# Attention then an MLP-mixer block on one core: when the second batch element's x is turned, where attention lies beside its token mixing, and two small reorderings

## The chip, the core and the metric

The kernel runs on one core of a Trainium2 chip. The core has TensorE (PE, with the weight load PEld beside it), VectorE (DVE), ScalarE (ACT), GpSimd (POOL) and SyncE (SP), whose queue issues nearly all DMAs. Each engine works through its own instructions in the order of the program, and waits by semaphores for the others. The metric is the device time in microseconds; a run's time is told beside the span of its profile.

## The reference

All in float32. First attention with normalized queries and keys, for 8 batch elements, 12 heads, 448 positions and 64 channels per head; then a mixer block on the result, which has 768 channels.

```python
q_n, k_n = (rmsnorm(q, g_q), rmsnorm(k, g_k))
scores = scale * np.matmul(q_n, k_n.transpose(0, 1, 3, 2))
attn = np.exp(scores - max); attn = attn / (sum(attn) + 1e-09)
out = np.matmul(attn, v)                      # (8, 12, 448, 64)

x = out.transpose(0, 2, 1, 3).reshape(8, 448, 768)
xt = x.transpose(0, 2, 1)
h = np.maximum(xt @ w_tok1, 0.0) @ w_tok2     # token mixing: 448 -> 256 -> 448
u = x + h.transpose(0, 2, 1)
h2 = np.maximum(u @ w_ch1, 0.0) @ w_ch2       # channel mixing: 768 -> 1536 -> 768
out = u + h2
```

## The kernel before

**Elements and pairs.** The work goes by batch element b = 0..7. Two heads make a pair, p = 0..47, six to an element; two pairs make a step group t = p // 2. While the mixer of element b runs, attention of element b + 1 runs beside it (`AHEAD = 1`). All instructions of PE, DVE, ACT and POOL stand in an order that the program itself writes out; only SP's queue is ordered by the framework. Work is kept in lists of items, each with a cost in us and a function that issues its instructions. `merge` (L27) weaves several lists into one in proportion to their costs; `run` issues them. `later(us, fn)` puts a function off until items of that cost have been run; the DMAs of x are issued so.

**Attention.** `att_step(g)` (L585) lists the items of step g; g = 4t + s, four steps s = 0..3 to a group of two pairs. The function `tiled` holds PE's part: `score` (L387, with the exponential of L391 on ACT), `values` (L460). After it stand, on DVE, `denominators` (at s = 0, L489 to L506, which write the attention result into `uT`), `group_sums` (L428: partial sums of the exponentials, 128x896), loads, then `behind` (reductions and roots for later pairs) and `turns`. `turns` are `turn_qk` (L361 to L369): queries and keys of the next pairs are transposed, on PE for pairs below 12 (`pre.plain`), on DVE above (L364), and the queries are multiplied by g on ACT (L367). At s = 2 pair n = 2t + 2 is turned, at s = 3 pair n + 1. Scores of step 4(t + 1) need both. From group `BIG` = 9 on attention is laid in larger blocks, `big_step`.

**Normalization.** `Start.square` (L1262 for pairs below 12, L1265 above) squares a pair's queries and keys on ACT into a buffer `sq`; `Start.reduce` (L1279) sums them on DVE. There are three such buffers: `sq_1` for pairs 1 and 3, `sq_2` (the front of the large tile `hb`) for 5 and 7, and `sq` for all others. `hb` holds queries and keys of the first pairs, and later the hidden layer of the channel mixing. `roots` makes inverse square roots by Newton steps, for pairs 2 to 11 on POOL (L1309 to L1312). `scale` (L349, DVE) applies them.

**x.** Token mixing needs x with positions on the partitions. For b > 0 `trans_x` (L744) transposes each of six blocks of `uT` in squares of 32 on DVE, three to a half; `send_x` (L712) writes a half with four DMAs into a DRAM buffer `xs`, 2 to 8 us later by the items' clock, and `load_x` (L719) reads it back 12 us later. `x_items(b, h)` lists half h. The buffer `xt` holds both halves and shares its memory with the sums `tu` of the channel mixing.

**Mixer.** `tok1` (L758) is the first product of the token mixing, four times four matmuls of 128x384, evicted by ACT (L761) into h1; `tok2` (L766) the second, six times two of 128x448, added into `uT` by DVE (L771). Both take turns in two PSUM banks, `m_ps`. The first halves of h1 come from x's half 0, the second from half 1. `moving_sums` make T1, T2 on DVE (L787, L788) and T3, T4 on POOL (L789, L790). Channel mixing of elements 1 to 7 uses seven products of quarter matrices in place of eight (`ch1` L882, 21 items; `ch2` L939, 21 items). Its weights come in units from DRAM (`load_units`, L813), some of which are sums of weight quarters.

**Element 0 prepares the weights.** In element 0 each of 36 weight stages is loaded (`raw`), converted on DVE and ACT (L263 to L308, five to six instructions, the last being L308), stored (L192) and used at once by `first_stage` (L854, four matmuls of 128x448); every sixth stage of the second layer is evicted by ACT and added to `uT` by POOL (L864). The sums of weights are made on POOL (L204 to L207): `some` for the first eight stages, `direct` for the last six from their stage tiles, and `sums`, 25 items that load, sum and send the other stages in turn. POOL's order behind the last stage is: six `direct` sums, two `sums`, the two L864 of the last stage, further `sums`, T3 and T4.

**Order around the change.** In element 0, attention steps 13 to 24 are merged with element 0's mixer; x's half 0 of element 1 is turned between steps 22 and 23. Then `last` is run: x's half 1, the last six stages, `direct`, `sums[:5]` and two output transposes (`turns`, L975, sent by L702). In element 1 `tok1` of half 0 is run with two more output transposes; then `tok1` of half 1, `tok2` and `ch1`, merged with `sums[5:20]`, are all woven into attention steps 25 to 36. From element 2 on attention blocks begin only with the first `ch1`.

The lines that decide this order:

```python
begin, early = merge(tok1_items(b, 1) + early[:3 * KC], left[2:]), early[3 * KC:]
if b == 1:
    early, double = merge(begin + early, sums[5:20]), merge(double, sums[20:])
    begin = []
early = begin + early + double
...
att = att_items(lo, lo + 10) + x_items(b + AHEAD, 0) + att_items(lo + 10, lo + per - (b == 1 and not shifted))
...
last = x_items(1, 1) + merge(last, direct + sums[:5], turns(b, y_order(b)[2:4]))
...
run(merge(att, early) + last)
```

`shifted` is a second form of the program, for large gains g, which does not run with these inputs.

Of the kernel before, what the change touches and what calls it, by code (L numbers as in the profile page):

```python
# [44 lines left out]
def whole(ctx, tc, shifted, pre, q, k, v, g_q, g_k, moe_w_tok1, moe_w_tok2, moe_w_ch1, moe_w_ch2, out):  # L45
# [386 lines left out]
    def on_pe(p):  # L432

        return shifted or p < NPAIR
# [150 lines left out]
    def att_step(g):  # L585


        t, s = divmod(g, 4)
        p = 2 * t
        pair = (p, p + 1)  # L590
        live = g < NG
        items = []

        def finish():
            if s == 0 and t:
                last = (p - 2, p - 1)
                for k in (NK - 2, NK - 1):
                    values(last, k)
            if live:
                for k in ((0,), (1, 2), (3, 4), (5, 6))[s]:  # L600
                    score(t, k)
            if s == 0 and t:
                if not on_pe(p - 1):
                    row_sums(t - 1)
                for i in last:
                    st.pop(("v", i))

        def tiled():
            if shifted:
                if live:  # L610
                    both_shifted()
            else:
                finish()
            if live and s == 3:
                for i in pair:
                    st.pop(("qkT", i))
            if inside:
                for fn in turns:
                    fn()
            if live and s and not shifted:  # L620
                for k in ((), (0,), (1, 2), (3, 4))[s]:
                    values(pair, k)

        def both_shifted():
            i = p + s // 2
            if s % 2 == 0:
                score_shifted(i)
                return
            for k in range(NK):
                values((i,), k)  # L630
            for k in range((NK + 1) // 2):
                st.pop(("e1", i, k))
            st.pop(("v", i))
            for part in denominators((i,)):
                part()

        n = p + 2
        ahead, behind, turns = [], [], []  # L640
        f = lambda fn, *pairs: [lambda i=i: fn(i, st) for i in pairs]
        scales = lambda n: [lambda i=i: scale(i) for i in (n, n + 1)]
        if g in (1, 5):
            ahead, behind = f(pre.square, g // 4 * 2 + 4), f(pre.reduce, g // 4 * 2 + 4)
        elif g in (2, 6):
            ahead, behind = f(pre.square, g // 4 * 2 + 5), f(pre.reduce, g // 4 * 2 + 5)
        elif g in (3, 7):
            behind = pre.roots(g // 4 * 2 + 4, st)
        elif g in (4, 8):
            behind = scales(g // 4 * 2 + 2)  # L650
        if live and n < NP:
            late = n < 2 * NPAIR + 2
            if t >= NPAIR // 2 and late:
                if s == 1:
                    ahead, behind = f(pre.square, n), f(pre.reduce, n) + f(pre.square, n + 1)
                elif s == 2:
                    behind = f(pre.reduce, n + 1) + pre.roots(n, st) + scales(n)
            elif t >= NPAIR // 2:
                a, b = f(pre.square, n) + f(pre.reduce, n), f(pre.square, n + 1) + f(pre.reduce, n + 1)
                behind = (a, b + pre.roots(n, st), scales(n), [])[s]  # L660
            now = {2: [] if pre.plain(n) else [n], 3: [n, n + 1] if pre.plain(n) else [n + 1]}.get(s, [])
            turns = [lambda q=q, i=i: turn_qk(q, i) for q in now for i in (1, 0)]

        inside = g < 2 * NPAIR
        items += [(0.3, fn) for fn in ahead]
        items.append((2.4 if s == 1 else 3.2, tiled))
        part = lambda fns, c=0.4: [(c, fn) for fn in fns]
        if s == 0 and t and not shifted:
            items += part(denominators((p - 2, p - 1)))
        if live and not on_pe(p):  # L670
            items += [(0.5, lambda k=k: group_sums(t, k)) for k in ((), (1, 2), (3, 4), (5, 6))[s]]

        if s == 0 and 5 < p + 1 < NP:
            items.append((0.0, lambda: load_v(p + 1)))
        if live and s == 1 and 5 < p + 2 < NP:
            items.append((0.0, lambda: load_v(p + 2)))
        js = []
        if live and s == 0:
            js = [n, n + 1] if pre.plain(p) else [n + 1]
        elif live and s == 3 and not pre.plain(n):  # L680
            js = [n + 2]
        items += [it for j in js if pre.first_slot + 2 <= j < NP
                  for it in part(pre.loads(j, st, nc.sync, nc.sync), 0.2 if pre.plain(j) else 0.6)]
        if g == 3:
            items += [it for j in (6, 7) for it in part(pre.loads(j, st, nc.sync, nc.sync), 0.2)]
        items += part(behind)
        if not inside:
            items += part(turns)
        if g == 4 * BIG - 1 and not shifted:
            items += part(pre.loads(n + 3, st, nc.sync, nc.sync), 0.3)  # L690
        return items
# [285 lines left out]
    def turns(b, cs, send=True):  # L977

        def one(cc):
            trans_y(b, cc)  # L980
            if send:
                later(2.0, lambda: send_y(b, cc, st.pop(("y", cc))))
        return [(0.3, lambda cc=cc: one(cc)) for cc in cs]

    def y_order(b):

        return [o * KC + m for m in ((0, 1, 2) if b else (2, 0, 1)) for o in range(2)]
# [6 lines left out]
    def x_items(b, h):  # L994
        return [(0.1, lambda j=j: trans_x(b, j)) for j in range(h * NC // 2, (h + 1) * NC // 2)]
# [108 lines left out]
    for b in range(B):  # L1104
        early, double = middle_items(b)
        if b == 0:
            early, last = first_items(
                tok1_items(0, 0) + x_items(0, 1) + tok1_items(0, 1) + early, double, some)
        else:
            if b > 1 and in_next(b - 1):  # L1110

                y, z = sends(b - 1, y_order(b - 1)[:4]), left
                left = [y[0], y[1], z[0], y[2], z[1], y[3]]
            run(merge(tok1_items(b, 0), left[:2]))
            begin, early = merge(tok1_items(b, 1) + early[:3 * KC], left[2:]), early[3 * KC:]
            if b == 1:
                early, double = merge(begin + early, sums[5:20]), merge(double, sums[20:])
                begin = []
            early = begin + early + double
            early, last = early[:-4], early[-4:]  # L1120
        lo = (b + AHEAD) * per + 1
        att = []
        if b + AHEAD < B and (shifted or b < 2):
            att = att_items(lo, lo + 10) + x_items(b + AHEAD, 0) + att_items(lo + 10, lo + per - (b == 1 and not shifted))
            if b and not shifted:
                ahead, block, beside, between = big_step(BIG, False)
                att += ahead + [block] + beside + between
        elif b + AHEAD < B:
            t = (b + AHEAD) * NPAIR // 2
            blocks = [big_step(t + i // 2, i % 2) for i in range(1, NPAIR + 1)]  # L1130
            blocks[4][3].extend(x_items(b + 1, 0))
            early = place(early, blocks, [near(early, at) for at in BLOCKS])
        if b == 0:
            last = x_items(1, 1) + merge(last, direct + sums[:5], turns(b, y_order(b)[2:4]))
        else:
            if b + 1 < B:
                last = merge(last, x_items(b + 1, 1))
            last += last_items(b)
        run(merge(att, early) + last)
        if b == 0:  # L1140
            load_units(0)
        left = turns(b, y_order(b)[4:])
# [5 lines left out]
class Start:  # L1148
# [105 lines left out]
    def square(self, p, st):  # L1254
        x, d = self.by_rows(p, st["qk", p])
        rows, n = x.shape[0], x.shape[1]
        if self.plain(p):

            parts = ((0, n),) if p else ((0, n // 2), (n // 2, n))
            sq = (self.sq_1 if p in (1, 3) else self.sq_2 if p in (5, 7) else self.sq)[0:rows]  # L1260
            for lo, hi in parts:
                self.nc.scalar.activation(out=sq[:, lo:hi, 0:d], in_=x[:, lo:hi], func=AF.Square)  # L1262
        else:
            sq = self.sq[:].rearrange("p r d -> p (r d)")[:, 0:n * d].rearrange("p (r d) -> p r d", d=d)
            self.nc.scalar.activation(out=sq, in_=x, func=AF.Square)  # L1265
        st["sq", p] = sq
# [130 lines left out]
```

## Time and profile before

| what | us |
|---|---|
| median of three runs | 1317.32 (1316.29 to 1317.63) |
| the profiled execution | 1318.47 |
| its span | 1316.7 |
| PE busy | 1269.7 |
| PE, channel mixing L882 and L939 | 201.8 + 150.7 and 339.6 |
| PE, scores L387 and values L460 | 145.4 and 132.7 |
| PE, token mixing L758 and L766 | 86.4 and 75.5 |
| DVE, partial sums L428: 90 of 1.219 | 109.7 |

The page gives one profiled execution. Lines are those of the kernel before; a group is named by line, engine, operation, and output and input tiles. "xN" counts instructions; a float32 matmul shows as two. A busy PE is not PE at its peak: its records stretch where the granted clock is lower. The chain that ended last is 75% PE and 2% DMA. In slices of a fortieth of the span PE is at 9 tenths or more but for the first, third, eighth, ninth and last:

```
PE   5989999889999999999999999999999999999997
DVE  6887688927774366644666267644666356433212
```

Element 0's mixer runs from about 85 to 271 us, element 1's from 271 to 440, and each of the next takes some 150 us.

### The profile page before, as it was taken

How to read it: one execution, taken by the hardware profiler on the slowest of the kernel's cores; microseconds unless marked ns; L12 is line 12 of the kernel's file. 1: busy time of each engine (PE TensorE's matmuls, PEld its weight loads, DVE VectorE, ACT ScalarE, POOL GpSimd, SP SyncE). 2: the span in 40 equal slices, each digit the busy share in tenths (PEclk: the TensorE clock that was granted, in tenths of full speed). 3: DMA queues.
4: the chain of work that ended last, by engine and by line, in shares of the span. 5: the costliest groups of instructions: out<-in, count | busy, mean ns of one | idle time of the engine just before them, and what ended most of it. 6: DMA issues, size and time to landing. Idle time of an engine off the chain costs nothing.

```text
span 1316.7 us, 20214 instructions
## 1 busy us (share of the span) xinstructions
PE 1269.7 (96%) x7408; PEld 933.5 (71%) x7408; DVE 763.8 (58%) x1205; ACT 372.6 (28%) x740; POOL 355.0 (27%) x575
## 2 busy tenths in 40 slices
PE   5989999889999999999999999999999999999997
PEld 3444444436788677796778767886787868797997
DVE  6887688927774366644666267644666356433212
ACT  5553333212332044302432033312333033200100
POOL 1203230355563122321232123321232123111220
PEclk9998999999999999999999999999999999999999
DMA  9664577889889767695648767585766964386554
GB/s 210 167 182 117 147 191 188 211 207 243 247 217 212 194 159 172 153 239 103 164 136 207 168 139 181 138 230 112 180 161 152 223 137 131 118 219 134 179 169 93
DMA packets 502449, 228.06 MB, mean 173 GB/s; under 512 B 374532, under 2 KB 464004, under 8 KB 502340
## 3 DMA queue, kind: packets, MB, share of 16 engines
q1 hardware_dynamic: 489218, 224.83, 68.6%
q10 hardware_dynamic: 12994, 1.84, 0.8%
q8 instruction: 61, 1.00, 0.3%
q14 instruction: 48, 0.39, 0.1%
q0 software_dynamic: 128, 0.00, 0.0%
HBM read 187.07 MB, written 39.52 MB: 172 GB/s over the span
## 4 chain that ended last, share of the span: by engine, by line
PE 75%; DMA 2%; DVE 1%; SPq 1%; POOL 0%; issue 0%; ACT 0%; DVEq 0%; POOLq 0%; ACTq 0%
PE m_ps L882 25%; PE m_ps L939 25%; PE s_ps L387 7%; PE o_ps L460 7%; PE m_ps L758 5%; PE m_ps L766 5%; PE d_ps L440 1%; DMA unit<-ws 1%; DMA x<-xs 0%; DMA qk_t<-in_k_dram 0%; DMA ws<-raw 0%; SPq L702 0%; DVE es L428 0%; DVE ms L1279 0%; DVE nt L1321 0%
## 5 line engine op out<-in xcount | busy, mean ns | idle before, releaser
L939 PE MATMUL m_ps<-hb,unit 128*128 128x224 f32 x1764 | 339.6, 353 | 2.2 <-DMA unit<-ws 1.5
L939 PEld LDWEIGHTS m_ps<-hb,unit 128*128 128x128 f32 x1764 | 332.2, 190 | 13.3 <-issue 10.9
L882 PE MATMUL m_ps<-tu,unit 128*128 128x224 f32 x1008 | 201.8, 355 | 0.3 <-DVE hb L887 0.3
L882 PEld LDWEIGHTS m_ps<-tu,unit 128*128 128x128 f32 x1008 | 189.0, 190 | 14.8 <-issue 8.5
L391 ACT ACTIVATE e<-s_ps 128x448 f32<-128x448 f32 x294 | 138.4, 549 | 188.2 <-PE s_ps L387 179.4
L387 PE MATMUL s_ps<-qkT 64*64 64x448 f32 x1260 | 145.4, 549 | 7.0 <-ACT qkT L367 4.2
L882 PE MATMUL m_ps<-uT,unit 128*128 128x224 f32 x756 | 150.7, 353 | 0.0
L882 PEld LDWEIGHTS m_ps<-uT,unit 128*128 128x128 f32 x756 | 142.5, 190 | 5.0 <-issue 4.1
L460 PE MATMUL o_ps<-e,v 64*64 64x448 f32 x1148 | 132.7, 547 | 0.1
L428 DVE TENSOR_TENSOR es<-es,e 128x896 f32<-128x896 f32 x90 | 109.7, 1219 | 19.6 <-ACT e L391 14.7
L948 POOL TENSOR_TENSOR uT<-uT,r 128x448 f32<-128x448 f32 (+1 forms) x56 | 57.8, 1041 | 231.4 <-DVE r L948 143.6
L887 DVE TENSOR_TENSOR r<-m_ps,r 128x448 f32<-128x448 f32 x63 | 39.2, 622 | 112.2 <-PE m_ps L882 59.0
L387 PEld LDWEIGHTS s_ps<-qkT 64*64 64x64 f32 x1260 | 45.6, 133 | 75.7 <-issue 59.4
L948 DVE TENSOR_TENSOR uT<-uT,m_ps 128x448 f32<-128x448 f32 (+1 forms) x70 | 33.8, 499 | 109.7 <-PE m_ps L939 109.7
L460 PEld LDWEIGHTS o_ps<-e,v 64*64 64x64 f32 x1148 | 46.4, 135 | 63.9 <-issue 60.3
L758 PE MATMUL m_ps<-x,w_sb 112*128 112x384 f32 x256 | 86.4, 494 | 5.5 <-DMA x<-xs 4.4
L887 POOL TENSOR_TENSOR hb<-r,r 128x448 f32<-128x448 f32 x21 | 24.4, 1163 | 241.5 <-ACT r L903 241.5
L766 PE MATMUL m_ps<-w_sb,h 128*128 128x448 f32 x192 | 75.5, 544 | 4.0 <-ACT h L761 2.5
L758 PEld LDWEIGHTS m_ps<-x,w_sb 112*128 112x128 f32 x256 | 49.1, 193 | 40.8 <-issue 8.5
L888 ACT ACTIVATE hb<-hb 128x448 f32<-128x448 f32 x63 | 36.3, 577 | 115.8 <-DVE hb L887 96.5
L1279 DVE TENSOR_REDUCE ms<-sq 128x28 f32<-128x896 f32 (+2 forms) x45 | 48.6, 1082 | 33.2 <-ACT sq L1265 30.5
L766 PEld LDWEIGHTS m_ps<-w_sb,h 128*128 128x128 f32 x192 | 35.4, 190 | 40.7 <-issue 26.4
(122 smaller groups left out, 1376.3 us busy)
## 6 DMA issues: line engine op xcount, KB each, us to landing
unit<-ws SPq DMA_DIRECT2D x294, 384.0 KB, 4.1
raw<-in_moe_w_ch_dram SPq DMA_DIRECT2D x72, 256.0 KB, 3.9
v<-in_v_dram SPq DMA_DIRECT2D x96, 112.0 KB, 3.8
xs<-xt SPq DMA_DIRECT2D x56, 168.0 KB, 4.6
x<-xs SPq DMA_DIRECT2D x14, 672.0 KB, 6.6
out_dram<-turned SPq DMA_DIRECT2D x168, 56.0 KB, 1.9
qk_t<-in_q_dram SPq DMA_DIRECT2D x144, 56.0 KB, 3.5
qk_t<-in_k_dram SPq DMA_DIRECT2D x144, 56.0 KB, 3.7
```

The source lines that it names most:

```text
L387: nc.tensor.matmul(out=pss[i][rows_of(i, a), 0:S], lhsT=qkT[h, 1, k * D:(k + 1) * D], rhs=qkT[h, 0, :], start=True, stop=True)
L391: nc.scalar.activation(out=e[:, i, :], in_=pss[i][:, 0:S], func=AF.Exp)
L428: nc.vector.tensor_tensor(out=es[:], in0=(es if k > 1 else st["e", t, 0])[:], in1=st["e", t, k][:], op=ALU.add)
L460: nc.tensor.matmul(out=st["o", p][a * D:(a + 1) * D, 0:S], lhsT=vt[rows, k * D:(k + 1) * D], rhs=e[rows, :], **kw)
L758: nc.tensor.matmul(out=ps[:, 0:HC], lhsT=w1_sb[0:R, c, jc * P:(jc + 1) * P], rhs=st["x", b, h][0:R, :, c, :], start=(c == 0), stop=(c == N ...
L766: nc.tensor.matmul(out=ps[:, 0:S], lhsT=st["h1", jc][:, cc * P:(cc + 1) * P], rhs=w2_sb[:, jc].rearrange("p c r -> p (c r)"), start=(jc == ...
L882: nc.tensor.matmul(out=ps[:, j * HS:(j + 1) * HS], lhsT=w[:, t, j, :], rhs=m, start=(t == 0), stop=(t == KC - 1))
L887: add = lambda e, o, x, y: e.tensor_tensor(out=o, in0=x, in1=y, op=ALU.add)
L888: relu = lambda x: nc.scalar.activation(out=x, in_=x, func=AF.Relu)
L939: nc.tensor.matmul(out=ps[:, j * HS:(j + 1) * HS], lhsT=st["w"](j, t), rhs=hb[:, HB[what], t, :], start=(t == 0), stop=(t == KF - 1))
L948: add = lambda e, o, x, y: e.tensor_tensor(out=o, in0=x, in1=y, op=ALU.add)
L1279: self.nc.vector.tensor_reduce(out=st["ms", p][:, p % 2, lo:hi], in_=sq[:, lo:hi], axis=AX_X, op=ALU.add)
```

## The change

Five edits. In `att_step`, at s = 3 and where the next pairs are turned on DVE, the turns stand ahead of the group sums instead of at the end. For element 1 the items `begin` (first mixing of half 1 and all second mixing) are run with `sums[5:9]` alone, without attention; the other sums of weights and `ch1` are woven together as before, but start with `sums[9:20]`. x's half 1 of element 1 is turned within step 24, behind its first five items (PE's part and the four of `denominators`), instead of in `last`. Attention beside element 1's mixer begins with six items of step 25 that are run at once, behind the token mixing. And the squares of pair 9 go into `sq_2`. The form `shifted` is left as it was.

```diff
+        soon = s == 3 and not inside and not pre.plain(n)
+        if soon:
+            items += part(turns)
         if live and not on_pe(p):
             items += [(0.5, lambda k=k: group_sums(t, k)) for k in ((), (1, 2), (3, 4), (5, 6))[s]]
...
-        if not inside:
+        if not inside and not soon:
             items += part(turns)
...
-            if b == 1:
+            if b == 1 and not shifted:
+                run(merge(begin, sums[5:9]))
+                early, double = merge(early, sums[9:20]), merge(double, sums[20:])
+                begin = []
+            elif b == 1:
                 early, double = merge(begin + early, sums[5:20]), merge(double, sums[20:])
                 begin = []
...
-            att = att_items(lo, lo + 10) + x_items(b + AHEAD, 0) + att_items(lo + 10, lo + per - (b == 1 and not shifted))
-            if b and not shifted:
+            att = att_items(lo, lo + 10) + x_items(b + AHEAD, 0)
+            if shifted:
+                att += att_items(lo + 10, lo + per)
+            elif not b:
+                step = att_step(lo + per - 1)
+                att += att_items(lo + 10, lo + per - 1) + step[:5] + x_items(1, 1) + step[5:]
+            else:
+                run(att[:6])
                 ahead, block, beside, between = big_step(BIG, False)
-                att += ahead + [block] + beside + between
+                att = att[6:] + att_items(lo + 10, lo + per - 1) + ahead + [block] + beside + between
...
-            last = x_items(1, 1) + merge(last, direct + sums[:5], turns(b, y_order(b)[2:4]))
+            last = x_items(1, 1) * shifted + merge(last, direct + sums[:5], turns(b, y_order(b)[2:4]))
...
-            sq = (self.sq_1 if p in (1, 3) else self.sq_2 if p in (5, 7) else self.sq)[0:rows]
+            sq = (self.sq_1 if p in (1, 3) else self.sq_2 if p in (5, 7, 9) else self.sq)[0:rows]
```

## The prediction

> **What bounds the kernel.** I read the page first: TensorE (PE) decides nearly everything, and what it does not fill is worth looking for.
>
> ```profile
> PE 1269.7 (96%) x7408; PEld 933.5 (71%) x7408; DVE 763.8 (58%) x1205; ACT 372.6 (28%) x740; POOL 355.0 (27%) x575
> ```
>
> Next the waits of PE, longest first (columns: who waits for whom, us in total, times, longest). Leaving out those at the start of the program, five rows remain that the change can touch; all lie before 305 us.
>
> ```profile
> PE m_ps L758 <- DMA x<-xs: 4.4, 1, 4.4
> PE s_ps L387 <- ACT qkT L367: 4.2, 2, 4.0
> ...
> PE s_ps L387 <- ACT x L738: 2.8, 1, 2.8
> PE m_ps L766 <- ACT h L761: 2.5, 1, 2.5
> PE m_ps L766 <- DVE uT L771: 1.5, 1, 1.5
> ```
>
> A wait costs more than its length. The busy times in stretches of 2 us show the granted clock (column after POOL) halved behind three of these gaps, while PE reads as busy:
>
> ```profile
> 100.00:102.00 2.00, 2.00 (x14) 1.20 (x12) 0.75 (x2) 2.00 (x5) 0.00 (x0) 0.50 0.05 10
> 102.00:104.00 2.00, 2.00 (x16) 1.09 (x10) 1.66 (x2) 0.69 (x2) 0.00 (x0) 0.50 0.88 273
> ...
> 240.00:242.00 2.00, 2.00 (x4) 0.92 (x3) 1.31 (x4) 0.26 (x1) 0.00 (x0) 0.53 1.11 286
> ...
> 284.00:286.00 2.00, 2.00 (x4) 1.06 (x4) 0.00 (x0) 0.00 (x0) 0.83 (x3) 0.50 1.18 311
> ...
> 296.00:298.00 2.00, 0.88 (x3) 0.50 (x4) 1.31 (x4) 1.93 (x7) 1.92 (x5) 1.00 1.00 397
> ```
>
> I price the lost clock as busy time times (1 - clock) over each such stretch: 2.9 us after the first gap (98 to 106: 0.25+1.0+1.0+0.68), 1.7 after the second (238 to 242: 0.76+0.94), 1.4 after the third (282 to 288: 0.30+1.0+0.14). None is lost behind the scattered gaps of 294 to 302, of at most 2.5 us each. So three places:
>
> - Place 1, 96.5 to 105.4: 2.8 + 2.9 = 5.7 us.
> - Place 2, 233 to 242: 4.0 + 1.7 = 5.7 us.
> - Place 3, 278 to 302: 4.45 idle to 285, 4.0 idle from 294 to 302, 1.4 clock = 9.9 us.
>
> Last the timeline of each place (start, length, engine, line, in brackets the idle time before and its releaser):
>
> ```profile
> 96.42 1.23 DVE L1279 TENSOR_REDUCE ms<-sq 112x16 f32<-112x1040 f32 x1
> 97.73 1.06 ACT L1262 ACTIVATE sq<-qk_t 112x1024 f32<-112x1024 f32 x1 [2.90 <-DVE ms L1279]
> 98.69 1.54 ACT L738 COPY x<-t_ps 112x512 f32<-112x512 f32 x3
> 99.31 2.50 PE L387 MATMUL s_ps<-qkT 64*64 64x448 f32 x10 [2.81 <-ACT x L738]
> ...
> 235.38 1.17 DVE L364 STREAM_TRANSPOSE qkT<-qk_t 128x448 f32<-128x448 f32 x2
> ...
> 237.30 0.59 PE L387 MATMUL s_ps<-qkT 64*64 64x448 f32 x2 [4.04 <-ACT qkT L367]
> ...
> 259.76 0.94 DVE L308 SCALAR_TENSOR_TENSOR stage<-raw 128x512 f32<-128x512 f32 x1
> ...
> 263.82 1.68 DVE L744 STREAM_TRANSPOSE xt<-uT 128x448 f32<-128x448 f32 x3
> ...
> 285.17 0.45 POOL L204 TENSOR_TENSOR raw<-raw 128x128 f32<-128x128 f32 x1 [13.83 <-DMA raw<-ws]
> ...
> 289.88 0.65 DVE L975 STREAM_TRANSPOSE turned<-uT 128x448 f32<-128x448 f32 x1 [23.33 <-POOL uT L864]
> ```
>
> To see here: at place 1 ACT's square of pair 9 waits for the reduction of pair 8 (one buffer, `sq`), and three copies behind it hold PE's score banks. At place 2 the keys of pair 13 are turned late. At place 3 x's half is late, and behind it POOL and DVE stand still, which hurts nobody yet.
>
> **What the Trainium skill says.** "TensorE: Matmul & The Clock Gate", section on the HAM clock gate: a window of about 3.4 us without work halves the clock, and about as long of sustained work restores it. The trace agrees for gaps of 4.0 and 4.4 us; it also shows halving after one of 2.8, so the boundary is not sharp here. "SBUF — State Buffer", "Who interferes with whom": some VectorE forms and GpSimd share a port pair, and the later one stands still. The trace agrees: beside POOL's additions at 252.1 to 255.0, L308 takes 1.64 us instead of 0.69 and L266 1.26 instead of 0.43. "DMA: Bandwidth & Descriptors", "Anatomy of one DMA": a semaphore wait happens on the issuing sequencer, not in a DMA engine; so one waiting transfer holds all behind it on SP. From 262 to 445 us SP waits 3.7 us in total at the loads of x for the stores of xs.
>
> **The change part by part.**
>
> *Pair 9's squares apart.* ACT's square no longer waits: its keys were issued by 87.8 us and land in about 4, so it runs at 94.9, behind the h eviction ending at 94.8. The copies follow at 96.0, and PE waits 0.1 us instead of 2.8, with no lost clock: PE is 5.7 us ahead at its next first-mixing products (99.7 for 105.45). But the second-mixing evictions (L771) stand on DVE behind the scaling of pair 8, which started at 110.93 after POOL's roots, themselves behind the reduction of pair 9 at 104.19. That reduction stands behind group sums and exponentials which follow a weight conversion of DVE ending at 99.9 (ACT L274 at 100.1): it moves 0.3 us at most. So PE waits near 111.5 for the first L771, and by 128 I have its lead at about 2. Beyond 128 the lead must also move DVE, which idled there only 0.49 + 0.64 + 1.31 us for PE, and later for loads. Bounds: 0 and -5.7; I take -1.3, about the last DVE wait.
>
> *Keys ahead of partial sums.* In step 23 two transposes (1.17) and the multiplication by g (0.67) go ahead of two sums of 1.08; with conversions between them they move from 235.4 to about 223.5, and PE needs the result at 233.3. The wait of 4.0 and 1.7 of clock go. What is late next are the stage products (L854): ten of them from 239.36 to 270.77, or (31.4 - 1.7)/10 = 2.97 each. From the back, stage 33 began at 270.77 - 3x2.97 = 261.9, and its conversion (L308) ended at 260.7: slack 1.2 us. For stages 32 and 31 slack is 3.3 and 5.0. DVE is 95% busy from 214 to 264, and this change makes it later, see next. The same swap in steps 27, 31 and 35 removes 0.16 us at most.
>
> *x's last half turned at once.* Three transposes (1.68) move from behind the last conversion to ahead of those of stages 31 to 35. PE, 5.7 us earlier, then waits 5.7 + 1.68 - 1.2 = 6.2 us in total, in pieces of about 2: place 2 returns +0.5 us if DVE's other work is as long as now. It can be shorter: POOL's additions move from beside conversions to beside the denominators (1.8 us of stretching), and two waits for raw loads (0.74 + 0.65) are in reach, since key loads stand otherwise between them on SP. Bounds +0.5 and -2.7; I take -0.5. With -1.3, first mixing of element 1 begins at 269.0 instead of 270.8.
>
> The four stores of xs and the load of x move ahead on SP. The load must stand behind four stores of weights, the last of which waits for stage 35's conversion (263.9), and behind the landing of xs (4.6 median after the last issue, near 261): issue at 265 to 266, landing 5.4 later (277.51 to 282.95 now), about 271. First mixing's second half wants it at 269.0 + 5.3 = 274.3: the 4.45 us idle and 1.4 clock go, 3 us to spare.
>
> *Token mixing alone.* The order of the changed kernel's instructions shows 16 first-mixing and 12 second-mixing products back to back on PE, attention from step 25 on behind them. No exponentials stand before the h evictions, no reductions and roots before the uT additions: the other 4.0 us of place 3 can go. The new cover is thin, though: DVE's additions stand behind two transposes of the output (L975), those behind POOL's L864, and those behind two weight sums (4 x 0.45 each), which wait for their loads. Call their landing t. First addition done: t + 3.6 + 2.2 (two L864) + 0.65 + 0.6 = t + 7.1. PE's third second-mixing product needs that bank at 269.0 + 10.7 + 2x1.6 + 0.1 = 283.0. SP issues these loads behind x, six stores of sums and an output, at about 271.5 (279.27 now), and they took 5.9: t = 277.4, a wait of 1.5. Bounds 0 and 9.3 (t as now, 285.2); I take +1.5.
>
> Behind that POOL makes T3 and T4 with five more sums among them, the last two waiting for loads behind eight output issues (8.9 us on SP now): done near 307.5, wanted near 307 by the fourth channel product. Bounds 0 and 4; I take +0.7. Keys for step 28: DVE reaches them near 308, wanted at 314. Attention's twelve steps now lie beside 35 products instead of those and the mixing: DVE's 91 us of 280 to 420 fall into 130, 70%, so no bound. Units for the first products are issued near 283 and land in 5.7, wanted at 293. At the end of the element the last block stands six matmuls nearer to the end, where PE lost 0.6 and 1.5 us; I cost it at nothing, bounds -2 and +2.
>
> Sum: -1.3 - 0.5 - 9.9 + 1.5 + 0.7 = -9.5 us. Afterwards every element runs as before, PE without a gap, so this reaches the end. The profiled execution took 1318.47 (span 1316.7), giving 1309.0; the median of the runs is 1317.32, 1.15 lower, so I forecast 1307.8.
>
> **Rivals.**
>
> *Everything comes through:* the lead of place 1 moves DVE with it, and DVE is relieved at place 2: -5.7 - 2.7 - 9.9 = -18.3, or less any new wait; about 1301. For it: DVE does idle for PE after 128. Against: the 95% before 264.
>
> *Nothing is gained, the wait moves to POOL:* t stays at 285.2, set by SP and full DMA (shares of 1.0 to 1.18 in 280 to 286). The wait is 9.3, with 1.5 of clock: of 11.0 gained elsewhere 0.2 is left, about 1317.1. For it: 23 us of DVE idling show how rigid this chain is. Against: SP stood behind x itself until 277.5.
>
> *Slower:* the same chain with t later still. The gain is gone at t = 285.4; from there each us of t is one us of PE, and at t = 288.5 the time is 1320.4. Loads would need over 14 us from when SP is free, or raw buffers that come free late because six sums' stores queue.
>
> **How the numbers follow.** Forecast 0.67 (its own range 1304 to 1312.5), everything through 0.13, nothing 0.12, slower 0.08. The range 1301 to 1316 takes in the forecast, most of the first rival and part of the second. A difference under 0.2% (2.6 us) is what a measurement here cannot tell from none. Faster by more: 0.67 + 0.13 + 0.02 = 0.82; within: 0.10; slower: 0.08.
>
> **What would show it.** Place 1: square at 95, PE without its wait at 99.3, but a wait for L771 near 111. Place 2: no wait for qkT; instead waits for stages 31 to 33 of 1 to 2.5 us, and first mixing at 267 to 271. Place 3: no wait for x; one for uT (L771's line) near 283, its length telling t. Wrong would be: attention steps 26 to 28 waiting for exponentials or keys, or a unit wait at 300 to 310.

## The result and the profile after

The changed kernel takes 1312.46 us (median; 1311.34 to 1313.78) where the kernel before takes 1317.63: a ratio of 0.9966, 95% interval 0.9954 to 0.9977. Beside other runs it was measured twice more, at 1313.48 against 1318.32 (0.9958 [0.9943, 0.9974]) and 1313.09 against 1317.92 (0.9962 [0.9946, 0.9977]). So it gains 4.8 to 5.2 us by the medians, 4.5 to 5.5 by the ratios; 9.5 were forecast. Of the kernel called "x late" below, one execution of twenty took 5081.66 us and is left out of its median. Lines of the changed kernel are 3 higher than before's from the scheduler's first edit on, 13 higher in the code that normalizes queries and keys.

The profiled execution took 1311.52 us, its span 1309.7. The busy times of its page (us, share, instructions) show 6 us less of PE, and otherwise the same work:

```profile
PE 1263.6 (96%) x7408; PEld 930.4 (71%) x7408; DVE 764.4 (58%) x1205; ACT 372.1 (28%) x740; POOL 352.8 (27%) x575
```

Its waits of PE, the program's start left out (us in total, times, longest):

```profile
PE m_ps L857 <- ACT r L866: 8.0, 2, 6.6
PE m_ps L769 <- DVE uT L774: 3.3, 3, 1.3
...
PE m_ps L942 <- DMA unit<-ws: 1.9, 1, 1.9
PE m_ps L942 <- DVE uT L951: 1.6, 1, 1.6
...
PE m_ps L885 <- DVE hb L890: 1.0, 1, 1.0
```

The waits for x by DMA (4.4), for turned keys (4.2), for the copies of x (2.8) and for h (2.5) are gone. One row is new and larger than any of them: 8.0 us for ACT's copies of a finished weight stage. The timeline shows where (start, length, engine, line; in brackets the idle time before and its releaser):

```profile
111.07 3.44 PE L769 MATMUL m_ps<-w_sb,h 128*128 128x448 f32 x8 [1.31 <-DVE uT L774]
...
235.39 0.43 DVE L263 TENSOR_SCALAR cv_sb<-raw 128x512 uint32<-128x512 uint32 x1 [1.59 <-DMA raw<-in_moe_w_ch_dram]
...
238.88 0.43 DVE L263 TENSOR_SCALAR cv_sb<-raw 128x512 uint32<-128x512 uint32 x1 [0.66 <-DMA raw<-in_moe_w_ch_dram]
...
245.52 1.69 DVE L747 STREAM_TRANSPOSE xt<-uT 128x448 f32<-128x448 f32 x3
...
249.01 0.43 DVE L266 TENSOR_SCALAR cv_sb<-raw 128x512 uint32<-128x512 uint32 x1
...
249.47 0.72 ACT L274 ACTIVATE cv_sb<-cv_sb,expo_c 128x512 uint32<-128x512 uint32 x1 [8.22 <-DVE cv_sb L266]
250.10 0.94 ACT L866 COPY r<-m_ps 128x448 f32<-128x448 f32 x2
250.66 20.05 PE L857 MATMUL m_ps<-hb,stage 128*128 128x448 f32 x48 [6.63 <-ACT r L866]
270.55 10.48 PE L761 MATMUL m_ps<-x,w_sb 112*128 112x384 f32 x32
...
278.24 0.45 POOL L204 TENSOR_TENSOR raw<-raw 128x128 f32<-128x128 f32 x1 [5.89 <-DMA raw<-ws]
...
282.93 0.65 DVE L978 STREAM_TRANSPOSE turned<-uT 128x448 f32<-128x448 f32 x1 [19.00 <-POOL uT L867]
...
285.23 6.28 PE L769 MATMUL m_ps<-w_sb,h 128*128 128x448 f32 x16 [1.19 <-DVE uT L774]
...
432.57 10.48 PE L761 MATMUL m_ps<-x,w_sb 112*128 112x384 f32 x32
```

Read the middle. PE finished stage 29 at 244.03. ACT could have copied its two banks then, but in ACT's queue one step of a weight conversion (L274) stands ahead of the copies, and its operand comes from DVE only at 249.44, behind two waits for raw weights (1.59 and 0.66), the denominators (241.0 to 245.5) and the three transposes of x. So PE stands for 6.63 us. In stretches of 2 us (busy us of PE, PEld, DVE, ACT, POOL; then the granted clock, the DMA share and GB/s) the clock is halved behind it, about 1.7 us more (20.05 us for six stages that take 18.35 at full clock):

```profile
248.00:250.00 2.00, 0.00 (x0) 0.00 (x0) 1.93 (x5) 0.53 (x1) 0.00 (x0) 0.50 0.91 271
250.00:252.00 2.00, 1.34 (x2) 0.84 (x3) 1.93 (x4) 1.89 (x4) 1.31 (x1) 0.50 1.21 245
252.00:254.00 2.00, 2.00 (x4) 0.86 (x3) 1.97 (x3) 0.05 (x1) 2.00 (x3) 0.50 0.71 138
254.00:256.00 2.00, 2.00 (x7) 1.02 (x6) 2.00 (x3) 0.67 (x1) 1.92 (x4) 0.95 1.03 190
```

At stage 26 PE was 7.6 us ahead of before (231.74 for 239.36); at element 1's first mixing it is 0.2 ahead (270.55 for 270.77). From there to element 2's first mixing it needs 162.0 us instead of 169.1. After that the two are alike: 151.0 us to element 3 in both.

### The profile page after: what moved, and what is told of

Read it like the earlier page. It is cut to its first block, busy times and chain, and to the rows that moved or that the text cites. A ratio compares the mean times of both kernels' runs of the same rounds, so it can differ in the third digit from the quotient of the medians.

```text
span 1309.7 us, 20218 instructions
## 1 busy us (share of the span) xinstructions
PE 1263.6 (96%) x7408; PEld 930.4 (71%) x7408; DVE 764.4 (58%) x1205; ACT 372.1 (28%) x740; POOL 352.8 (27%) x575
## 4 chain that ended last, share of the span: by engine, by line
PE 79%; DVE 8%; DMA 5%; SPq 3%; issue 2%; ACT 1%; POOL 1%; DVEq 0%; ACTq 0%; POOLq 0%
PE m_ps L885 25%; PE m_ps L942 24%; PE o_ps L460 8%; PE s_ps L387 8%; PE m_ps L769 5%; PE m_ps L761 5%; DVE raw L264 1%; PE m_ps L857 1%; PE d_ps L440 1%; DVE raw L281 1%; DMA raw<-in_moe_w_ch_dram 1%; DMA qk_t<-in_k_dram 1%; PE m_ps L440 1%; DVE cv_sb L263 1%; DVE stage L308 1%
## 5 line engine op out<-in xcount | busy, mean ns | idle before, releaser
L387 PE MATMUL s_ps<-qkT 64*64 64x448 f32 x1260 | 142.0, 545 | 0.0
L857 PE MATMUL m_ps<-hb,stage 128*128 128x448 f32 x144 | 57.2, 556 | 8.0 <-ACT r L866 8.0
```

Source lines behind the costliest of these rows:

```text
L387: nc.tensor.matmul(out=pss[i][rows_of(i, a), 0:S], lhsT=qkT[h, 1, k * D:(k + 1) * D], rhs=qkT[h, 0, :], start=True, stop=True)
L857: nc.tensor.matmul(out=ps, lhsT=a[:, o + 2 * half, :], rhs=natural(half)[:, :, t, :] if wide else u[:, half * KC + t, :], start=(t == 0 an ...
```

## The experiments

Two times tell them apart: the start of element 1's first mixing (M1) and of element 2's (M2), of the one profiled execution each. Rows with the same time of before share its runs; lines of these kernels differ by a few from the changed one's.

| kernel | median us | before beside it | ratio, 95% | M1 | M2 |
|---|---|---|---|---|---|
| before, two profiles | | | | 270.77, 268.77 | 439.88, 438.28 |
| changed | 1312.46 | 1317.63 | 0.9966 [0.9954, 0.9977] | 270.55 | 432.57 |
| changed, again | 1313.48 | 1318.32 | 0.9958 [0.9943, 0.9974] | 271.43 | 434.25 |
| changed, third | 1313.09 | 1317.92 | 0.9962 [0.9946, 0.9977] | 269.43 | 430.40 |
| squares only | 1316.40 | 1318.02 | 0.9981 [0.9972, 0.9991] | 268.41 | 438.60 |
| keys only | 1316.76 | 1318.02 | 0.9986 [0.9977, 0.9995] | 266.48 | 436.38 |
| element 2's part only | 1314.72 | 1318.02 | 0.9975 [0.9958, 0.9992] | 271.71 | 435.06 |
| changed, x late | 1316.39 | 1318.02 | 0.9985 [0.9975, 0.9996] | 263.88, 266.67 | 433.50, 432.83 |
| changed without keys | 1314.03 | 1317.92 | 0.9966 [0.9949, 0.9983] | 269.21 | 435.29 |
| ScalarE's order | 1314.37 | 1318.32 | 0.9968 [0.9952, 0.9984] | 268.09 | 433.41 |
| x between | 1317.53 | 1318.32 | 0.9992 [0.9982, 1.0003] | 267.29 | 434.34 |
| x between, GpSimd's order | 1317.55 | 1318.32 | 0.9994 [0.9985, 1.0003] | 267.56 | 436.87 |
| both orders | 1311.67 | 1317.27 | 0.9955 [0.9940, 0.9970] | 269.01 | 431.82 |
| GpSimd's order | 1310.60 | 1317.27 | 0.9945 [0.9933, 0.9958] | 271.28 | 429.74 |
| GpSimd's order, again | 1311.51 | 1317.92 | 0.9949 [0.9934, 0.9965] | 270.93 | 431.07 |
| both orders, fewer sums | 1313.00 | 1317.92 | 0.9959 [0.9946, 0.9971] | 266.34 | 433.11 |

**Each part alone.** Squares only:

```diff
-            sq = (self.sq_1 if p in (1, 3) else self.sq_2 if p in (5, 7) else self.sq)[0:rows]
+            sq = (self.sq_1 if p in (1, 3) else self.sq_2 if p in (5, 7, 9) else self.sq)[0:rows]
```

> The kernel before with one edit alone: the tenth pair's squares in a buffer of their own. Theory A (a lead of TensorE is lost at the stage conversions only when ScalarE's queue stands in conversions that VectorE has not reached, so what counts is how much earlier VectorE itself comes; with this edit alone VectorE and TensorE both move by about 3 us): first mixing product of element 1 about 2.6 us earlier than the 270.8 of before, time 2 to 3.5 us less. Rival B (VectorE's conversions alone absorb every lead): mixing within 1 us of 270.8, time within 1 us of before.

M1 came 2.4 us earlier than in the first profile of before, and the time fell by 1.6 us in medians, 2.5 by the ratio. By M1 that is theory A; but before's second profile has M1 only 0.4 later, and the gain in time is little against a spread of 6 us of the single runs.

Keys only: the two hunks of `soon`, nothing else.

> The kernel before with one edit alone: the keys turned ahead of the partial sums. Theory A: the wait for the turned keys (5.7 us at 230 us) goes, and the whole of it comes back as one wait of about 5 us for ScalarE's copies of a weight stage at about 250 us, with TensorE's clock halved behind it: mixing at 270.3 to 271.5, time within 1 us of before. Rival (each edit is worth its own wait): mixing at about 265 to 268, time 3 to 5.7 us less.

Theory A missed. M1 came 4.3 us earlier, as the rival had it: with x turned late, the keys' lead passes the conversions (80 records of stage products in one piece, 236.31 to 266.6). Yet the time fell by only 1.3 to 1.9 us, as x then came late (PE waits 4.9 us for it). So the conversions do not take the lead by themselves.

Element 2's part only: the changed kernel without those two edits.

> The changed kernel without the squares' buffer and without the keys' earlier turn: only element 2's part, x turned at once and token mixing with no attention beside it. Theory A: this is all of the gain that the changed kernel keeps: from the first mixing product of element 1 to that of element 2 162 us (before 169.1), time 6 to 7 us below before and within 1.5 us of the changed kernel. Rival (the squares and the keys carry part of the gain after all): 2 us or more slower than the changed kernel.

M1 to M2 is 163.35 us, within 1.4 of what was expected, but the time fell by 3.3 us only, 6 to 7 being expected, and it lies 2.3 above the changed kernel's first median, 1.2 to 2.2 by the ratios, which settles neither expectation. Squares and keys together are worth something like that; singly they were worth 2.5 and 1.9, so the parts do not add up.

The fourth corner, the changed kernel with `soon = False`:

> The changed kernel without the keys' earlier turn; the squares' buffer and element 2's part are kept. Theory A (a lead won ahead of 250 us is lost at the conversions and at the chain behind GpSimd, so the keys' turn brings nothing where x is turned early): mixing of element 1 at 270 to 272, element 2 at 432 to 435, time within 1 us of the changed kernel on this chip. Rival (the edits add up): 1.5 to 3 us slower than the changed kernel.

It takes 0.9 us more than the changed kernel beside it, with ratios of 0.9966 and 0.9962: beside the early turn of x the keys' turn is worth nothing that these runs can tell. M1 (269.21) and M2 (435.29) missed the expected bands a little.

**Where the lead goes.** The changed kernel with x's last half turned where before turned it:

```diff
-                att += att_items(lo + 10, lo + per - 1) + step[:5] + x_items(1, 1) + step[5:]
+                att += att_items(lo + 10, lo + per - 1) + step
...
-            last = x_items(1, 1) * shifted + merge(last, direct + sums[:5], turns(b, y_order(b)[2:4]))
+            last = x_items(1, 1) + merge(last, direct + sums[:5], turns(b, y_order(b)[2:4]))
```

> The changed kernel with the last half of x of element 2 turned where the kernel before turned it, so that token mixing stands alone but does not find x early. Theory A: the transfer that brings x lands at about 282 us or later, token mixing waits some 6 us for it and runs on at a halved clock for a while: 5 to 8 us slower than the changed kernel, about the time of before. Rival (taking the attention out from beside token mixing is what gains, and x's place is of no matter): within 1 us of the changed kernel.

```profile
245.69 18.35 PE L857 MATMUL m_ps<-hb,stage 128*128 128x448 f32 x48 [0.51 <-ACT r L866]
263.88 5.33 PE L761 MATMUL m_ps<-x,w_sb 112*128 112x384 f32 x16
276.83 7.16 PE L761 MATMUL m_ps<-x,w_sb 112*128 112x384 f32 x16 [7.63 <-DMA x<-xs]
```

In this timeline of PE the wait of 6.63 us is 0.51, and M1 comes 6.7 us before the changed kernel's. Its timeline of DVE has the operand of L274:

```profile
244.03 0.43 DVE L266 TENSOR_SCALAR cv_sb<-raw 128x512 uint32<-128x512 uint32 x1
```

It comes 5.0 us earlier than in the changed kernel's first profile. Of these 1.7 are the transposes of x and 2.2 the two waits for raw weights, which are absent here; for the rest, taking three items out of the step also changed where some conversions and square roots are woven in. So the early turn of x is part of what took the lead, and this run does not separate it from the weaving. Here the lead is lost one step later, to x itself (7.63 us and 1.8 of clock), so that M2 is only 0.9 later than in the changed kernel. The median is 3.9 us higher all the same, 2.5 by the ratios. Neither expectation held: x landed at 276.8 and not at 282, and the loss lies between the two. A second profile of it:

> The kernel with x late once more, for a second profile, as its median of 1316.6 lies 4 us above the run that was profiled. Theory A (x late costs its wait and a halved clock behind it, by an amount that goes with when the transfer lands): mixing again at 263 to 265, a wait for x of 7 to 11 us, and a time that is longer by about as much as x lands later than 282.5. Rival: the wait for x as before and the difference elsewhere.

M1 was 266.67, beyond the band; the wait 4.57, shorter than the band; M2 432.83. Neither theory: the lead was smaller and the wait with it, and M2 stayed. Both profiled executions (1312.65 and 1311.49) lie 3.7 and 4.9 us below this kernel's median, so its profiles do not show why that is higher.

The kernels themselves once more, to see what one profile is worth:

> The kernel before once more, for a second profile. Theory A (the first profile of before is typical in its places): mixing of element 1 at 270 to 272, of element 2 at 439 to 441.5, with waits of 3.5 to 4.5 us for turned keys and 4 to 5 for x. Rival (one profile is not typical of the kernel): a place differs by more than 2 us.

> The changed kernel again, on the chip of the experiments beside it. Theory A (the order of the instructions sets where the lead is lost): first mixing product of element 1 again at 269 to 271.5, with one wait of 5 to 7 us for ScalarE's copies of a weight stage at about 250; time 4 to 6 us below before. Rival (two late transfers of raw weights at 235 and 239, 2.3 us together, were chance of that one run and made the loss): VectorE's waits for raw weights under 0.5, mixing at 267 to 268.5.

> The changed kernel beside the others of this call: a ratio to before of 0.995 to 0.997, its median 4 to 6 us below before; mixing at 270.5 to 271.5, element 2 at 432.5 to 434.5.

Before: M1 2.0 us earlier, and x waited for 2.76 instead of 4.44; M2 1.6 earlier, the span about the same (1316.4 for 1316.7): theory A's bands for M1, M2 and x were missed, by up to 1.2 us. Changed: the wait for ACT's copies at 250 us was 4.58 and 5.11 us, the first just below theory A's band. VectorE waited 0.17 for raw weights in the second profile, so the late transfers of the first were chance; they can account for about 2 of its 6.63 us, and 4.6 remain without them. In the third profile M1 (269.43) and M2 (430.40) came 1 and 2 us before the expected bands, while the ratio was as expected. The spans are 1309.7, 1311.2 and 1307.5: one profile of this kernel stands for its time only within some 2 us either way.

ScalarE's order: one L274 (and nothing else on any engine) goes behind the copies.

```diff
+            if i == HELD + 1:
+                convert_second(HELD - 1)
             convert_bits(i - 2)
...
-            if 0 <= i - 1 < len(chunks):
+            if 0 <= i - 1 < len(chunks) and i != HELD:
                 convert_second(i - 1)
...
+    HELD = BEFORE + 24
```

> The changed kernel with one ScalarE instruction of a conversion put behind the copies of the stage before it, and nothing else moved. Theory A (the 6.6 us wait is ScalarE's queue, but the conversions behind it bind too): the wait for the copies falls below 1 us, TensorE then waits for converted weights of VectorE instead, in pieces of 1 to 4 us; mixing at 268 to 269.5 instead of 270.55, time 0.5 to 2 us less than the changed kernel. Rival B (the conversions alone set it): mixing stays at 270 to 271. Rival C (ScalarE's queue is all of it): mixing at 264 to 265.

Its timeline of ACT, then that of PE:

```profile
244.28 0.53 ACT L865 COPY r<-m_ps 128x448 f32<-128x448 f32 x1 [2.18 <-PE m_ps L856]
245.78 0.53 ACT L865 COPY r<-m_ps 128x448 f32<-128x448 f32 x1 [0.97 <-PE m_ps L856]
...
250.31 0.72 ACT L274 ACTIVATE cv_sb<-cv_sb,expo_c 128x512 uint32<-128x512 uint32 x1 [3.15 <-DVE cv_sb L266]
```

```profile
250.94 17.31 PE L856 MATMUL m_ps<-hb,stage 128*128 128x448 f32 x40 [2.24 <-DVE stage L308]
268.09 10.48 PE L760 MATMUL m_ps<-x,w_sb 112*128 112x384 f32 x32
...
285.19 7.87 PE L768 MATMUL m_ps<-w_sb,h 128*128 128x448 f32 x16 [3.61 <-DVE uT L773]
```

The copies now wait for PE, PE waits 2.24 us for DVE's conversion, and M1 is 268.09: theory A, and rivals B and C are out, as far as one profile tells. Yet the time did not fall (0.9968 for 0.9958), where theory A had it 0.5 to 2 us less. PE goes on at 285.19, where it went on in the changed kernel (285.23, 285.22; in the third profile 284.01), and the 2.5 us have become a wait of 3.61 with a halved clock behind it.

**The wall at 285 us.** What PE waits for there ends a chain: the weight sums' loads land (POOL's L204 at 278.24 in the changed kernel's timeline above), two weight sums follow, then the last two additions to uT (L867), two output transposes of DVE (L978), and DVE's first addition of the token mixing, which frees PE's bank. The next run keeps this chain. x's half turned behind the conversions of all stages but the last, its stores due at once and its load 4 us on, instead of 2 and 12:

```diff
-            items += [(0.0, convert[5 + k][1]) for k in range(len(convert) - 5) if begins(k) == j]
+            for k in range(len(convert) - 5):
+                if begins(k) == j:
+                    items.append((0.0, convert[5 + k][1]))
+                    if k == len(convert) - 5 - 3 and not shifted:
+                        items += x_items(1, 1)
```

> The changed kernel with the last half of x turned behind the last full conversion but one instead of ahead of three of them, and its stores and its load sent off at once. Theory A: the lead is kept (mixing at 263 to 265.5 as in the run with x late), x comes within 1 us of when it is needed, and then token mixing's second half waits 5 to 8 us for sums of VectorE that stand behind GpSimd's additions to uT, which stand behind its waits for weights: time within 1.5 us of the changed kernel. Rival: no such wait, 5 to 7 us less than the changed kernel.

M1 is 267.29, x came in time, and PE waited 4.72 us and went on at 285.50: the wall as expected, the lead and the wait a little smaller. The median missed: 4 us above the changed kernel, though the profiled execution (1314.0) was at its level. With GpSimd's additions of stage 35 ahead of the weight sums as well (`sums[2:5]` run behind `last`):

> The kernel with x turned later, with GpSimd's last two additions to uT also put ahead of the weight sums that wait for transfers. Theory A: mixing at 263 to 265.5, no wait over 2 us in token mixing, element 2's first mixing product at 425 to 428 instead of 432.6: 5 to 7 us less than the changed kernel. Rival (the weights' sums or their transfers are next, as they come no earlier than before): element 2 at 430 or later, at most 2 us less.

No wait for sums over 1 us, but M2 is 436.87: theory A missed, and the rival's numbers held by another cause. VectorE turned x 2.7 us later than in the run before, so that x came 3.0 us late; it had waited 1.62 us for raw weights at 239 us, ahead of anything that this edit moves, so most of that is chance. The weight sums' loads, which moved with their items, landed at 282.1 instead of 278.5; 2.7 of that is VectorE's lateness too. So this profile says little on the edit itself. The next kernels start from the changed one and leave those loads ahead (`one` is split into its load and its rest): only the additions move.

```diff
-            last = x_items(1, 1) * shifted + merge(last, direct + sums[:5], turns(b, y_order(b)[2:4]))
+            last = x_items(1, 1) * shifted + merge(last, direct + sums[:2] + [(1.0, lambda i=i: one(i, rest=False)) for i in (2, 3)], turns(b, y_order(b)[2:4]))
+            last += [(0.0, lambda i=i: one(i, load=False)) for i in (2, 3)] + sums[4:5]
```

> The changed kernel with both queues mended: the one ScalarE instruction put behind the copies (as in the run with ScalarE's order), and GpSimd's last two additions to uT put ahead of the two weight sums that wait for a transfer landing at 278 us. Theory A (the lead that comes back at the conversions is lost again at 285.2 us, where VectorE's sums wait for GpSimd): mixing at 267.5 to 269, the wait for the sums in token mixing under 1 us instead of 3.6, element 2's first product at 427 to 430, time 3 to 5.5 us less than the changed kernel. Rival (the transfers of weight sums hold the later products anyway): element 2 at 432 or later, time within 1 us of the changed kernel.

> The changed kernel with GpSimd's order alone mended. Theory A: without the lead of 2.5 us at the conversions there is only the wait of 0.3 to 1.2 us in token mixing to gain; mixing at 270.5 to 271.5, element 2 0.3 to 1.5 us earlier than 432.6 to 434.3, time within 1.5 us of the changed kernel. Rival (GpSimd's late additions delay more than that wait shows): 2 us or more faster.

GpSimd's order alone, its timeline of POOL and then that of PE:

```profile
272.75 2.22 POOL L864 TENSOR_TENSOR uT<-uT,r 128x448 f32<-128x448 f32 x2
278.11 0.46 POOL L204 TENSOR_TENSOR raw<-raw 128x128 f32<-128x128 f32 x1 [3.14 <-DMA raw<-ws]
```

```profile
271.28 10.49 PE L758 MATMUL m_ps<-x,w_sb 112*128 112x384 f32 x32
281.60 9.18 PE L766 MATMUL m_ps<-w_sb,h 128*128 128x448 f32 x24
...
429.74 10.48 PE L758 MATMUL m_ps<-x,w_sb 112*128 112x384 f32 x32
```

The additions run at 272.75 instead of 281.77, token mixing has no gap, and M2 is 2.8 us earlier than in the changed kernel's first profile although M1 is 0.7 later. From M1 to M2 it needs 158.5 us, and 160.1 in a second profile, where the changed kernel's three need 161.0 to 162.8. That is the rival: more than the wait of 0.3 to 1.2 that it removes. The wait for DVE at 349 us (0.99) goes with it, and is 0.5 in the second profile. With both orders M1 is 2.3 earlier and M2 2.1 later than that, and M2 falls between theory A's band and the rival's, with a time 0.4 to 1.5 us below the changed kernel's by the ratios; PE waits for GpSimd's sums of uT:

```profile
307.43 4.05 PE L884 MATMUL m_ps<-tu,unit 128*128 128x224 f32 x20 [2.00 <-POOL tu L791]
```

GpSimd's order beside the changed kernel on one chip, and both orders with two weight sums moved behind those sums (`sums[5:7]` and `sums[7:20]` for `sums[5:9]` and `sums[9:20]`):

> The changed kernel with GpSimd's order alone mended, again, beside the changed kernel. Theory A (GpSimd's late additions delay VectorE and with it several later waits): element 2 at 429.5 to 431, 2 to 3.5 us below the changed kernel in time. Rival (the first run was a good one): within 1.5 us of the changed kernel.

> Both queues mended, and two of the weight sums that stood ahead of the sums of GpSimd for the channel products put behind them. Theory A (in the run with both mended the lead was lost to GpSimd at 307 us, 2.0 us, and to VectorE at 348, 1.1 us): the wait at 307 goes, element 2 at 428.5 to 430.5 instead of 431.8, time 1 to 3 us less than with both mended. Rival (the lead is taken by the next wait once more): element 2 at 431 or later.

GpSimd's order alone is 1.6 us below the changed kernel, between the two expectations; by its first run's ratio it was 1.7 to 2.8 below. Its intervals overlap those of the changed kernel, so the sign is likely and not certain; it is the fastest kernel here. The last kernel has the earliest start of all that find x in time, no wait at 307, and gains nothing. Its timeline of PE:

```profile
266.34 10.49 PE L760 MATMUL m_ps<-x,w_sb 112*128 112x384 f32 x32
...
324.70 1.72 PE L459 MATMUL o_ps<-e,v 64*64 64x448 f32 x4 [3.31 <-DMA v<-in_v_dram]
...
433.11 5.33 PE L760 MATMUL m_ps<-x,w_sb 112*128 112x384 f32 x16
```

The rival: the lead is taken by the next wait, here a load of v. Over all kernels with token mixing alone M1 lies between 263.9 and 271.7, M2 between 429.7 and 436.9, and the earlier M1 does not go with the earlier M2.

## Where the forecast held and where it failed

*Place 1.* As written, and larger: the wait at 99 us and its lost clock went, PE was 7.3 us ahead at its first-mixing products where 5.7 was worked out, waited for L774 at 111 and 116 us (1.31 and 0.84), and had 4.7 us of lead at 120 us where about 2 was taken; DVE's scaling of pair 8 came 2.73 us earlier (108.20 for 110.93), where a move of DVE was doubted.

*Place 2.* The wait for the keys went, and the lead at stage 26 was 7.6 us (5.6 and 7.4 in the other two profiles), the 2 + 5.7 of the forecast. **Here the step failed**: "PE, 5.7 us earlier, then waits 5.7 + 1.68 - 1.2 = 6.2 us in total, in pieces of about 2", with no term for lost clock. The three profiles show 8.0, 6.4 and 6.6 us of waiting for ACT's copies, one piece of it of 4.6 to 6.6, and 20.05 to 21.00 us for the six stages behind it, which take 18.35 without. The total of the waits was near the forecast's; one long piece in place of several short ones added 1.7 to 2.7 us of halved clock. The forecast counted only DVE's conversions; it left out that the copies that free PE's banks stand in ACT's queue behind one of them. With that one instruction moved, the waits for conversions were 2.24 in one run and 1.00, 0.24 and 1.23 in another (1.70, 0.24 and 1.23 in a third), and M1 was 268.09 and 269.01 (266.34 in the third) for the 269.0 forecast. Without, M1 is 269.4 to 271.4: of 1.8 us of gain forecast, the mean of the three leaves 0.3 against the first profile of before, and none against the mean of its two.

*Place 3.* The working held. x came in time, t (the landing of the weight sums' load) was 278.24, 278.23 and 277.01 for 277.4, and PE's third second-mixing product started at t + 7.0 in each, for t + 7.1 forecast. It did so in the four other profiles that find x in time and keep this order of GpSimd (the squares and keys left out, the keys left out, ScalarE's order, x between). M1 to M2 shrank by 7.1, 6.3 and 8.1 us against 169.1 before, for 7.7. The wait for GpSimd's T3 and T4, priced at 0.7, was nothing; instead 1.0 us was lost to DVE at 349 in the first profile, and 1.6 and 1.9 at the element's end where 0.6 and 1.5 had been: "I cost it at nothing".

*The rest.* The forecast's profiled execution, 1309.0, compares with 1311.52, 1313.02 and 1309.41: 2.3 us are missing on average. M1, 1.5 later on average than the 269.0 forecast, is most of that in the sum. It is not shown to cost as much time: with the one instruction moved M1 came in earlier, PE waited longer at t + 7.0, and the time did not fall. From there to the median it took off 1.15, as the kernel before had shown; but the changed kernel's medians lie 0.5 to 3.7 us above its profiled executions. That term, 1.15 the one way and 1.7 on average the other, is 2.8 us off and so larger than the failed step. The executions of one set spread over 2 to 9 us, so chance may be part of it. The record has the mean granted clock of every execution, and in each set the longer ones tend to have the lower clock: with x late from 1312.20 us at 0.995 to 1320.15 at 0.988, in the changed kernel's second set from 1308.59 at 0.996 to 1316.42 at 0.992. A thousandth of the clock is about 1.3 us of such a span (an estimate from these spans), so lost clock can be most of the difference. Where the longer executions lose it no profile shows, and it stays open; so do the 3.5 to 5 us between profile and median of the kernels with x late and with x between.

*The rivals.* "Everything comes through" is out: DVE did move, but ACT's queue, and then the wall at t + 7, took the lead. "The wait moves to POOL" is right in mechanism, and 0.3 to 1.2 us in size instead of 9: t came 278.24, 278.23 and 277.01 where before's two profiles have 285.17 and 281.44, as SP no longer stood behind x (see the last section). Even a better start would not have helped: where PE comes to its third second-mixing product before t + 7.0, it waits there.

## What to carry to other kernels

Before adding up what several edits save, follow the engine that is set free to the next thing it must wait for, and look in the queue of the engine that releases it: a short copy behind one instruction that waits elsewhere held TensorE for 4.6 to 6.6 us here, the counted conversions for 2.2 to 3.2 in all once that instruction was moved. A lead is worth time only up to the next event that does not move with it: here, mending what stood between the landing at t and the product brought 1.6 to 2.8 us, as far as the runs can tell, and the earlier start alone none. And take a second profile of both kernels before believing a difference of 2 us.

## What the runs showed of the hardware

The landing t of the weight sums' loads hardly moved with TensorE: 277.0 to 279.1 us in twelve of the fourteen profiles with token mixing alone, whose M1 lies between 263.9 and 271.4. (The other two are element 2's part only, 280.4, and GpSimd's order with x between, 282.1.) It goes with VectorE and with what stands on SP. In the changed kernel's three profiles it lies 15.4 to 15.5 us behind the end of VectorE's last conversion (262.85, 262.77 and 261.53). In the six profiles in which x is turned last, with its stores and its load ahead on SP, it lies 20.3 to 21.3 behind it. In the changed kernel the DMA share is 0.94 from 250 to 270 us and 0.87 from 270 to 290.

Whether a wait halves the clock is not a matter of its length alone. The changed kernel's second profile, then both orders, then x late, and x late again; each is the product group after the first wait for ACT's copies:

```profile
224.34 6.28 PE L857 MATMUL m_ps<-hb,stage 128*128 128x448 f32 x16 [1.82 <-ACT r L866]
```

```profile
224.48 7.98 PE L856 MATMUL m_ps<-hb,stage 128*128 128x448 f32 x16 [1.91 <-ACT r L865]
```

```profile
223.51 6.28 PE L857 MATMUL m_ps<-hb,stage 128*128 128x448 f32 x16 [3.08 <-ACT r L866]
```

```profile
224.10 9.30 PE L857 MATMUL m_ps<-hb,stage 128*128 128x448 f32 x16 [3.25 <-ACT r L866]
```

Sixteen such records take 6.28 us at full clock. Behind a wait of 1.91 us they took 1.7 longer, behind one of 3.08 no longer, behind one of 3.25 3.0 longer. The granted clock (behind POOL's column) of both orders, then of x late, shows it:

```profile
226.00:228.00 2.00, 2.00 (x4) 0.97 (x3) 2.00 (x2) 0.00 (x0) 1.46 (x1) 0.50 0.88 281
```

```profile
224.00:226.00 2.00, 2.00 (x7) 1.07 (x6) 2.00 (x2) 0.51 (x1) 2.00 (x2) 1.00 1.07 320
```

What else decides it these runs do not show. The Trainium skill ("TensorE: Matmul & The Clock Gate", on the HAM clock gate) gives a window of about 3.4 us without work. The measurements decide: in this kernel a wait of 1.9 us cost almost as much again and one of 3.1 nothing, so a forecast has to price a wait of 2 to 4 us both ways, with the clock lost and without.
